# A decode block's backward pass: stores issued by SP, loads by GpSimd, and the turn's row products in another order

## The chip, the cores and the metric

The kernel runs on one core of a Trainium2 chip. A core has five engines with their own instruction queues: TensorE (PE), VectorE (DVE), ScalarE (ACT), GpSimd (POOL) and SyncE (SP, which only issues transfers and waits). Sixteen DMA engines move data between HBM and the on-chip memory (SBUF); a transfer is issued by SP, ScalarE or GpSimd, and the issuing engine works through its queue in order. The metric is the device time of one execution in microseconds. A profile of one execution is taken beside the timed runs.

## The reference

One token of a transformer block with adaptive layer norm, forward and backward. Cut to what matters here:

```python
mod = (silu(c) @ w_mod).reshape(1, 6, 1, -1)           # sa, ca, ga, sb, cb, gb
h = layernorm(x) * (1 + ca) + sa
q = (h @ wq) per head                                   # 32 heads, 192 each
p = softmax(q @ k_cache.T * 192 ** -0.5)                # 8192 keys per head
x1 = x + ga * ((p @ v_cache) @ wo)
h = layernorm(x1) * (1 + cb) + sb
out = x1 + gb * (h + gelu(layernorm(h) @ w3) @ w4)      # the mixing part before w3 falls away for one token
# outputs: out, and by jax.vjp the gradients of
# x, k_cache, v_cache, wq, wo, w3, w4, c, w_mod
```

All tensors are bfloat16. K and V are 32 x 8192 x 192 each, 100.7 MB; so are dK and dV. For one query, dV of a head is the outer product of p and the head's gradient do (8192 x 192), and dK the outer product of dS and q. dWo, dWq, dWmod, dW3 and dW4 are outer products of two vectors too.

## The kernel before

**Forward.** For each head, K is loaded in two halves (tiles of 128 x 32 x 192, 1.5 MB), multiplied by q on VectorE, summed by TensorE, and softmaxed; K scaled by p (tile EK) goes through TensorE with V. That gives the output o and, in MA_all and MB_all, the products that later yield dq without a second pass over K. All loads are issued by SP.

**The turn.** Between the last head's forward and the first head's backward lies a chain of small steps on 5 or 12 columns: the sum ao_c over the heads' products with Wo (`fwd_ao_add`), two layer norms (`ln_cols`), u = h W3, the GELU and its derivative, du, dn2 = du W3^T, two layer norm gradients (`ln_bwd_cols`), dao, the first pair's do, its broadcast do_pb, and the first dV. Beside this chain some bigger work is spread, in an order written by hand:

- `dg_some(n)`: row products on VectorE, one for each of the 12 blocks of W4 (a 128 x 640 product with a sum, into a column of d_g; needed for du);
- `w3T_pe(n)` and `w3T_act(n)`: 15 groups of transposes of W3 on TensorE into PSUM banks, and their copies by ScalarE (needed for dn2). Banks "a" and "b" hold one group, a tile of "s" two; which group takes which is `g % 6`;
- `woT_some(n)`: 4 groups of transposes of the last pair's Wo (needed for do).

These are called from the fills of the layer norms (`ln1_fill`, `ln2_fill`, `lb2_fill`), which run while the chain waits for a sum over partitions on TensorE.

**Backward.** One step i for each head, from the last to the first. In it (lines of the profile):

1. `bwd_mult` (L132, L1000): V of the head times do_pb on VectorE, in place, and sums by TensorE into dP_ps;
2. `ring_load`: loads into a ring of 6 tiles that hold V and, five times, a batch of Wo; a load waits for the reader of the tile that it replaces. The first three are issued ahead of the backward pass;
3. `bwd_dv` of the next head: 20 of 32 rows on ScalarE (L1005), 12 on VectorE (L983), and a store (L1008) for each half;
4. side work: the row products with Wo (L917), `job_dwo` in steps 1 to 16 (three products on ScalarE at L1050 and a store, L1069), `job_dw4` in steps 17 to 20 (L1058), `job_dw3` (L1063), and from step 9 on the pieces of Wq and Wmod: a load (`job_outer_load`, L1096), a product and stores of dWq and dWmod (wq_o, wm_o, L1125);
5. `bwd_ds` and `bwd_dk` (L983, L1035): the two halves of dK, each with a store.

dK, dV and the forward's K share five tiles ("big"); late in the backward more tiles join. All loads are issued by SP (`nc.sync`), all stores by GpSimd (`st2 = nc.gpsimd`). Each queue is in program order: a store that waits for its producer holds up the stores behind it, a load that waits for a free tile holds up the loads behind it.

Of the kernel before, what the change touches and what calls it, by code (L numbers as in the profile page):

```python
# [20 lines left out]
def kernel(  # L21
# [26 lines left out]
    nc = tc.nc  # L48
# [16 lines left out]
    P = 128  # L65
# [6 lines left out]
    JH = J // 2  # L72
# [21 lines left out]
    def bank(tag, bufs=1, name=None, n=512):  # L94
        return psum[0].tile([P, n], FP32, tag=tag, name=name or "ps_" + tag, bufs=bufs)
# [32 lines left out]
    def ccol(n, name, dtype=FP32):  # L128
        return const.tile([P, n], dtype, name=name)
# [195 lines left out]
            return (0, P), (P, DH), 0, 3 * (h // 2), 3 * (h // 2) + 1  # L325
        return (DH - P, DH), (0, DH - P), DH - P, 3 * (h // 2) + 2, 3 * (h // 2) + 1

    def load_v(pool, h, t, slot):
        tl = pool.tile([P, JH, DH], BF16, name="V_sb", tag=f"v{slot}")
        nc.sync.dma_start(out=tl, in_=V_hd[h][:, t * JH : (t + 1) * JH, :])  # L330
        return tl

    def load_fwd(h, t, kind):
# [205 lines left out]
    def dg_some(n):  # L539
        f0 = dg_next[0]  # L540
        f1 = min(f0 + n, NFC)
        dg_next[0] = f1
        for f in range(f0, f1):
            j0 = 5 * D + 12 * P + f % 2 * D
            jk = w_t[2][:, j0 : j0 + D]
            nc.vector.tensor_tensor_reduce(out=jk, in0=w4n(f, 0, D), in1=dbo_bc, scale=1.0, scalar=0.0, op0=ALU.mult, op1=ALU.add, accum_out=d_g[:, f : f + 1])
# [142 lines left out]
    def w3T_pe(n):  # L689
        for g in range(w3T_next[0], min(w3T_next[0] + n, NG3)):  # L690
            b = g % 6
            if b in (0, 2):
                w3T_ps[g] = bank("s", 2, "t_ps", SB[0])
                w3T_ps[g + 1] = w3T_ps[g][:, 512:1024]
            elif b > 3:
                w3T_ps[g] = bank("ab"[b - 4], name="t_ps")
            for k in range(4):
                f, i = divmod(4 * g + k, NDC)
                nc.tensor.matmul(w3T_ps[g][:, k * P : (k + 1) * P], lhsT=w3n(i, f * P, (f + 1) * P), rhs=ident_bf, start=True, stop=True)
        w3T_next[0] += n  # L700
# [18 lines left out]
    fwd_kvK(hl - 1, 3, st[hl - 1])  # L719
    nc.scalar.copy(out=kb_sb, in_=kb_ps[:, 0 : 2 * DH])  # L720
    fwd_ao_add(HH - 2, sl_["sm"])
    dg_some(1)
    fwd_ao_add(HH - 1, sl_["sm"], 420)
    fek_cm.__exit__(None, None, None)
    fsm_cm.__exit__(None, None, None)
# [13 lines left out]
    for i in range(1, HQ):  # L739
        ring += [("v", HS[i], t) for t in range(2) if (i, t) != (1, 1)]  # L740
        if i % 2 == 1 and 0 < i // 2 < len(BATCHES):
            ring.append(("w", i // 2, 0))
    ring_n, freed = [0], set()
    NR = 6

    def ring_slot(n):
        return (3, 4, 5, 2, 0, 1)[n % NR]

    def ring_load():
        while ring_n[0] < len(ring) and (ring_n[0] < 3 or ring_key(ring_n[0] - NR) in freed):  # L750
            kind, k, t = ring[ring_n[0]]
            slot = ring_slot(ring_n[0])
            pool = bv if slot > 2 else fv
            ring_n[0] += 1
            if kind == "v":
                V_b.setdefault(k, {})[t] = load_v(pool, k, t, slot)
            else:
                load_wo(k, pool.tile([P, JH, DH], BF16, name="V_sb", tag=f"v{slot}"))

    def load_wo(k, tl):  # L760
        lo, n = PS[BATCHES[k][-1]], len(BATCHES[k])
        tl = tl.rearrange("p j d -> p (j d)")[:, 0 : 3 * n * D].rearrange("p (c r) -> p c r", r=D)
        nc.sync.dma_start(out=tl, in_=wo_v[:, 3 * lo : 3 * (lo + n), :])
        for hp in range(lo, lo + n):
            for cc in range(3):
                wo_src[hp, cc] = tl[:, 3 * (hp - lo) + cc, :]
# [3 lines left out]

    ring_load()
    big_order[:] = [0, 4, 1, 4, 1, 2, 3, 4, 1, 2, 3, 4, 0, 1] + [2, 3, 4, 0, 1] * HQ
    st2 = nc.gpsimd

    do_pb = {}
    q_pb = {}
# [12 lines left out]
        bwd_pf_dve(h)  # L789

    def ln1_fill(k):
        if k == 0:
            dg_some(1)
        else:
            w3T_pe(4)
            w3T_act(4)

    def ln2_fill(k):
        w3T_pe(1 + 2 * k)
        dg_some(1)  # L800

    x1_c = ccol(NDC, "x1_c")
    mul(x1_c, ao_c, ga)
# [50 lines left out]
    for f in range(NFC):  # L854
        for i in range(NDC):
            nc.tensor.matmul(dn2_ps[:, i : i + 1], lhsT=w3T(f * NDC + i), rhs=du_bf[:, f : f + 1], start=False, stop=(f == NFC - 1), skip_group_check=True)
    bwd_pf_act(HS[0])
    dn2 = ccol(NDC, "dn2")
    dve_copy(dn2, dn2_ps[:, 0:NDC])
    mid_ps = {"h2": aux_ps[:, 32 : 32 + NDC]}  # L860
# [4 lines left out]
                nc.tensor.matmul(mid_ps["h2"][:, r : r + 1], lhsT=w4n(f, r * P, (r + 1) * P), rhs=g_bf[:, f : f + 1], start=False, stop=(f == 6), skip_group_check=True)  # L865

    def lb2_fill():
        woT_some(4)

    dhb = ccol(NDC, "dhb")  # L870
    ln_bwd_cols(dn2, n2_c, r2, dbo_c, dhb, "lb2", lb2_fill)
    dn1 = ccol(NDC, "dn1")
    mul(dn1, dhb, cb1)
    dx1 = ccol(NDC, "dx1")
    ln_bwd_cols(dn1, n1_c, r1, dy_c, dx1, "lb1")
    dao_bf = ccol(NDC, "dao_bf", BF16)
    mul(dao_bf, dx1, ga)
    bwd_pf_dve(HS[0])
# [175 lines left out]
    def job_dw4(k):  # L1054
        o = bso.tile([P, 3, D], BF16, name="dw4", tag="so")
        for cc in range(3):
            tsc(o[:, cc, :], dbo_bc, g_f[:, 3 * k + cc : 3 * k + cc + 1], 0)
        st2.dma_start(out=out_7[3 * k * P : 3 * (k + 1) * P, :].rearrange("(c p) r -> p c r", p=P), in_=o)  # L1058

    def job_dw3(i):  # L1060
        o = bso.tile([P, F], BF16, name="dw3", tag="so")
# [3 lines left out]
    def job_dwo(hp):  # L1065
        o = bso.tile([P, 3, D], BF16, name="dwo", tag="so")
        for cc in range(3):
            tsc(o[:, cc, :], dao_bc, o_col_f[:, 3 * hp + cc : 3 * hp + cc + 1], 0)
        st2.dma_start(out=out_5[3 * hp * P : 3 * (hp + 1) * P, :].rearrange("(c p) r -> p c r", p=P), in_=o)  # L1069

    side = {}
    side_cm = []
# [249 lines left out]
```

## Time and profile before

| | |
|---|---|
| median of three runs | 1381.44 us (1379.0 to 1411.71) |
| the profiled execution | 1382.5 us, span 1380.7 us |
| busy: TensorE / VectorE / ScalarE / GpSimd | 852.1 / 1070.6 / 945.0 / 112.0 us |
| moved over DMA | 569.25 MB, mean 412 GB/s |
| read from HBM / written to HBM | 341.51 / 225.91 MB |
| HBM rate, 36 to 500 us (forward) | 417 GB/s |
| HBM rate, 566 to 572 us (in the turn) | 96 GB/s |
| HBM rate, 660 to 1080 us (backward) | 425 GB/s |

The span is from the first to the last instruction; times within it are counted from its start. "Busy" of an engine counts its instructions' durations. The DMA share is the mean busy share of the 16 DMA engines. A wait is put down to what ended it. The forward pass ends at about 540 us, the first store of dV is issued at 570.93 us.

### The profile page before, as it was taken

How to read it: one execution, taken by the hardware profiler on the slowest of the kernel's cores; microseconds unless marked ns; L12 is line 12 of the kernel's file. 1: busy time of each engine (PE TensorE's matmuls, PEld its weight loads, DVE VectorE, ACT ScalarE, POOL GpSimd, SP SyncE). 2: the span in 40 equal slices, each digit the busy share in tenths (PEclk: the TensorE clock that was granted, in tenths of full speed). 3: DMA queues.
4: the chain of work that ended last, by engine and by line, in shares of the span. 5: the costliest groups of instructions: out<-in, count | busy, mean ns of one | idle time of the engine just before them, and what ended most of it. 6: DMA issues, size and time to landing. Idle time of an engine off the chain costs nothing. (4 is left out here: it accounts for less than half of the span.)

```text
span 1380.7 us, 28348 instructions
## 1 busy us (share of the span) xinstructions
PE 852.1 (62%) x11655; PEld 672.8 (49%) x11655; DVE 1070.6 (78%) x1273; ACT 945.0 (68%) x2586; POOL 112.0 (8%) x203
## 2 busy tenths in 40 slices
PE   3699999999999999738645744234332435324242
PEld 3577777777777777726534532123221323213131
DVE  3588778878887886799997977857757859579695
ACT  1388777877877884866786657576864866557781
POOL 0000000000000000111101101111111111021010
PEclk9799999999999998566666666666766666666665
DMA  9999999999999999899999999999999999999997
GB/s 392 416 415 420 419 418 420 421 411 418 418 419 407 418 417 376 311 381 422 409 425 427 427 426 428 428 426 427 420 423 421 407 427 426 429 423 406 429 428 311
DMA packets 73167, 569.25 MB, mean 412 GB/s; under 512 B 6862, under 2 KB 19918, under 8 KB 32846
## 3 DMA queue, kind: packets, MB, share of 16 engines
q1 hardware_dynamic: 48592, 341.52, 60.2%
q0 software_dynamic: 24416, 225.92, 38.9%
q8 instruction: 91, 1.49, 0.4%
q14 instruction: 38, 0.31, 0.1%
q10 hardware_dynamic: 30, 0.00, 0.0%
HBM read 341.51 MB, written 225.91 MB: 411 GB/s over the span
## 5 line engine op out<-in xcount | busy, mean ns | idle before, releaser
L1005 ACT ACTIVATE dV<-do_pb,PF 128x192 bf16<-128x192 bf16 x1246 | 434.6, 440 | 108.7 <-DMA out_dram<-dK 60.6
L1000 PE MATMUL dP_ps<-V_sb,ident_bf 128*128 128x256 bf16 (+1 forms) x1584 | 229.2, 319 | 246.8 <-DVE V_sb L132 246.8
L407 ACT ACTIVATE EK<-K_sb,E_f 128x192 bf16<-128x192 bf16 x992 | 351.1, 442 | 4.1 <-PE kb_ps L302 2.8
L1000 PEld LDWEIGHTS <-ident_bf 128*128 128x128 bf16 x1584 | 179.3, 116 | 296.3 <-issue 169.1
L983 DVE TENSOR_TENSOR dK<-dS,q_pb 128x6144 bf16<-128x6144 bf16 x64 | 213.2, 3354 | 59.4 <-DMA out_dram<-dK 54.0
L132 DVE TENSOR_TENSOR prod<-K_sb,q_pb 128x6144 bf16<-128x6144 bf16 x64 | 214.4, 3349 | 3.6 <-DMA K_sb<-in_A_k_cache_dram 3.6
L132 DVE TENSOR_TENSOR V_sb<-V_sb,do_pb 128x6144 bf16<-128x6144 bf16 (+1 forms) x66 | 212.0, 3253 | 0.0
L432 PE MATMUL ps_a<-EK,V_sb 128*128 128x193 bf16 x1984 | 192.9, 249 | 1.9 <-DMA V_sb<-in_A_v_cache_dram 1.9
L432 PEld LDWEIGHTS <-V_sb 128*128 128x128 bf16 x1984 | 165.6, 99 | 19.5 <-issue 12.7
L983 DVE TENSOR_TENSOR dV<-P2h,do_pb 128x2304 bf16<-128x2304 bf16 (+2 forms) x67 | 88.8, 1353 | 50.1 <-DMA out_dram<-dV 40.4
L414 DVE TENSOR_TENSOR EK<-K_sb,P2h 128x1536 bf16<-128x1536 bf16 x124 | 117.5, 949 | 0.0
L1008 POOL DMA_DIRECT2D out_dram<-dV x68 | 37.0, 545 | 934.9 <-DVE dV L983 607.7
L443 PE MATMUL ps_b<-EK,V_sb 128*64 128x193 bf16 x1984 | 109.3, 253 | 0.0
L372 PE MATMUL S_ps<-prod,ident_bf 64*64 64x256 bf16 x3072 | 101.7, 280 | 11.9 <-DVE prod L132 11.9
L372 PEld LDWEIGHTS <-ident_bf 64*64 64x64 bf16 x3072 | 86.7, 111 | 32.6 <-issue 28.3
L443 PEld LDWEIGHTS <-V_sb 128*64 128x64 bf16 x1984 | 81.9, 110 | 19.7 <-issue 16.1
L393 ACT ACTIVATE E_f<-sm_ps,negm 128x64 f32<-128x64 f32 x31 | 9.7, 314 | 104.4 <-DVE negm L391 104.4
L376 DVE TENSOR_REDUCE S<-S_ps 128x128 f32<-128x1024 f32 x32 | 39.2, 1224 | 49.0 <-PE S_ps L372 49.0
L449 PE MATMUL kb_ps<-EK,hot_bf 128*32 128x384 bf16 x992 | 64.8, 339 | 0.0
L1050 ACT ACTIVATE wq_o<-wq_bc,ha_f 128x1536 bf16<-128x1536 bf16 x12 | 18.4, 1564 | 44.4 <-DMA out_dram<-wq_o 44.4
L191 PE MATMUL bc_ps<-ident_bf,dq_bf 128*128 128x128 bf16 x48 | 6.4, 304 | 66.6 <-ACT do_pb L195 65.5
L1035 POOL DMA_DIRECT2D out_dram<-dK x64 | 35.3, 552 | 136.7 <-DVE dK L983 95.1
(266 smaller groups left out, 805.8 us busy)
## 6 DMA issues: line engine op xcount, KB each, us to landing
V_sb<-in_A_v_cache_dram SPq DMA_DIRECT2D x125, 1536.0 KB, 14.2
K_sb<-in_A_k_cache_dram SPq DMA_DIRECT2D x64, 1536.0 KB, 14.4
out_dram<-dK POOLq DMA_DIRECT2D x64, 1536.0 KB, 23.0
out_dram<-dV POOLq DMA_DIRECT2D x61, 1536.0 KB, 22.4
wq<-in_A_wq_dram SPq DMA_DIRECT2D x3, 2560.0 KB, 33.9
wo_t<-in_A_wo_dram SPq DMA_DIRECT2D x16, 480.0 KB, 14.9
out_dram<-dwo POOLq DMA_DIRECT2D x16, 480.0 KB, 18.2
wq<-in_A_wq_dram SPq DMA_DIRECT2D x4, 1920.0 KB, 28.3
```

What stands on the lines that cost most here:

```text
L132: nc.vector.tensor_tensor(out=out, in0=a, in1=b, op=ALU.mult)
L372: nc.tensor.matmul(st["S_ps"][c0 : c0 + 64, r, t * JH : (t + 1) * JH, :], lhsT=ident_bf[64 * r : 64 * r + 64, 64 * r : 64 * r + 64], rhs=p ...
L376: nc.vector.reduce_sum(out=st["S2"], in_=st["S_ps"], axis=AX.X)
L407: nc.scalar.activation(out=st["EK"][q][:, jj, 0:DH], in_=K_st[h, t][:, r * JQ + jj, :], func=ACT.Copy, scale=st["E_f"][:, j : j + 1])
L414: nc.vector.tensor_tensor(out=EK[:, NA:JQ, 0:DH].rearrange("p j (d r) -> p j d r", r=2), in0=K_st[h, t][:, r * JQ + NA : (r + 1) * JQ, :]. ...
L432: nc.tensor.matmul(st["A_ps"][:, 0:n], lhsT=V_sb[:, r * JQ + jj, a0:a1], rhs=EK[:, jj, 0:n], start=(q == 0 and jj == 0), stop=(q == 3 and ...
L443: nc.tensor.matmul(st["B_ps"][g : g + 64, 0:n], lhsT=V_sb[:, r * JQ + jj, b0:b1], rhs=EK[:, jj, 0:n], start=(q == 0 and jj < 2), stop=(q = ...
L449: nc.tensor.matmul(kb_ps[g : g + 32, 0 : 2 * DH], lhsT=hot_bf[:, HQ - 1 - h : 2 * HQ - 1 - h], rhs=EK[:, jj : jj + 2, 0:DH], start=(h == 0 ...
L983: nc.vector.tensor_tensor(out=o.rearrange("p j (d r) -> p j d r", r=2), in0=pairs[:, :, None, :].to_broadcast([P, n, NP2, 2]), in1=vec.rea ...
L1000: nc.tensor.matmul(bst[h]["dP_ps"][:, t * JH + r : t * JH + r + n, :], lhsT=ident_bf, rhs=V_sb[:, :, k * DS : (k + 1) * DS], start=(k == 0 ...
L1005: nc.scalar.activation(out=o[:, jj, :], in_=vec_of(do_pb, h), func=ACT.Copy, scale=bst[h]["PF"][:, t * JH + jj : t * JH + jj + 1])
L1008: st2.dma_start(out=dV_hd[h][:, t * JH + r0 : t * JH + r1, :], in_=o[:, r0:r1, :])
```

## The change

The stores of dK, dV, dW3, dWq, dWmod and of the small outputs move from GpSimd's queue to SP's; the loads of the ring from the fourth on, all loads of Wo for the backward pass, and those of Wq and Wmod move from SP's queue to GpSimd's. The stores of dWo and dW4 stay on GpSimd. In the turn, one row product leaves the place between the two additions to ao_c, one leaves the first fill of ln2, and one joins the second fill of ln1; W3's groups of transposes take the PSUM banks in another order (a, b first, then the double ones); Wo's transposes are spread over three places: one group ahead of the copy of dn2, two in the fill of the first layer norm gradient, one in that of the second.

```diff
-    def load_v(pool, h, t, slot):
+    def load_v(pool, h, t, slot, eng=None):
         tl = pool.tile([P, JH, DH], BF16, name="V_sb", tag=f"v{slot}")
-        nc.sync.dma_start(out=tl, in_=V_hd[h][:, t * JH : (t + 1) * JH, :])
+        (eng or nc.sync).dma_start(out=tl, in_=V_hd[h][:, t * JH : (t + 1) * JH, :])
...
     def w3T_pe(n):
             b = g % 6
-            if b in (0, 2):
+            if b in (2, 4):
...
-            elif b > 3:
-                w3T_ps[g] = bank("ab"[b - 4], name="t_ps")
+            elif b < 2:
+                w3T_ps[g] = bank("ab"[b], name="t_ps")
...
     fwd_ao_add(HH - 2, sl_["sm"])
-    dg_some(1)
     fwd_ao_add(HH - 1, sl_["sm"], 420)
...
+    ldq = nc.gpsimd
...
-                V_b.setdefault(k, {})[t] = load_v(pool, k, t, slot)
+                V_b.setdefault(k, {})[t] = load_v(pool, k, t, slot, ldq if n >= 3 else nc.sync)
...
     def load_wo(k, tl):
-        nc.sync.dma_start(out=tl, in_=wo_v[:, 3 * lo : 3 * (lo + n), :])
+        nc.gpsimd.dma_start(out=tl, in_=wo_v[:, 3 * lo : 3 * (lo + n), :])
...
-    st2 = nc.gpsimd
+    st2 = nc.sync
...
     def ln1_fill(k):
-        if k == 0:
-            dg_some(1)
-        else:
+        dg_some(1)
+        if k == 1:
             w3T_pe(4)
             w3T_act(4)
...
     def ln2_fill(k):
         w3T_pe(1 + 2 * k)
-        dg_some(1)
+        dg_some(k)
...
     bwd_pf_act(HS[0])
+    woT_some(1)
     dn2 = ccol(NDC, "dn2")
...
     def lb2_fill():
-        woT_some(4)
+        woT_some(2)
+
+    def lb1_fill():
+        woT_some(1)
...
-    ln_bwd_cols(dn1, n1_c, r1, dy_c, dx1, "lb1")
+    ln_bwd_cols(dn1, n1_c, r1, dy_c, dx1, "lb1", lb1_fill)
...
     def job_dw4(k):
-        st2.dma_start(out=out_7[3 * k * P : 3 * (k + 1) * P, :].rearrange("(c p) r -> p c r", p=P), in_=o)
+        nc.gpsimd.dma_start(out=out_7[3 * k * P : 3 * (k + 1) * P, :].rearrange("(c p) r -> p c r", p=P), in_=o)
...
     def job_dwo(hp):
-        st2.dma_start(out=out_5[3 * hp * P : 3 * (hp + 1) * P, :].rearrange("(c p) r -> p c r", p=P), in_=o)
+        nc.gpsimd.dma_start(out=out_5[3 * hp * P : 3 * (hp + 1) * P, :].rearrange("(c p) r -> p c r", p=P), in_=o)
...
     def job_outer_load(name, view, lo, n):
-        nc.sync.dma_start(out=w, in_=view[:, :, lo : lo + n])
+        ldq.dma_start(out=w, in_=view[:, :, lo : lo + n])
```

More of the change, by code (lines that the diff above doesn't have):

```diff
@@ L750, in ring_load @@
         while ring_n[0] < len(ring) and (ring_n[0] < 3 or ring_key(ring_n[0] - NR) in freed):
-            kind, k, t = ring[ring_n[0]]
-            slot = ring_slot(ring_n[0])
+            n = ring_n[0]
+            kind, k, t = ring[n]
+            slot = ring_slot(n)
             pool = bv if slot > 2 else fv
```

## The prediction

> **What bounds the kernel now.** I read the page's slices of DMA first, then a table of stretches, then waits and issues, and last the turn's timeline.
>
> ```profile
> DMA  9999999999999999899999999999999999999997
> DMA packets 73167, 569.25 MB, mean 412 GB/s; under 512 B 6862, under 2 KB 19918, under 8 KB 32846
> q1 hardware_dynamic: 48592, 341.52, 60.2%
> q0 software_dynamic: 24416, 225.92, 38.9%
> ```
>
> The first line is the busy share of the 16 DMA engines in 40 slices, in tenths: full from start to end, with a notch at the turn and one at the end. All loads are in the first queue (issued by SP), all stores in the second (issued by GpSimd); together they fill the engines. By stretches (start and end in us, the length, busy time of the five engines, granted clock, DMA share, GB/s):
>
> ```profile
> 36.00:500.00 464.00, 433.91 (x7864) 342.60 (x7857) 370.59 (x559) 352.91 (x1040) 0.00 (x0) 0.97 1.01 417
> 540.00:566.00 26.00, 22.78 (x419) 20.74 (x419) 16.81 (x76) 13.86 (x30) 0.00 (x0) 0.61 0.97 376
> 566.00:572.00 6.00, 4.36 (x93) 3.89 (x91) 3.52 (x10) 3.63 (x12) 0.88 (x2) 0.50 0.27 96
> 572.00:600.00 28.00, 15.18 (x250) 14.49 (x251) 27.69 (x32) 19.93 (x58) 4.61 (x9) 0.62 0.97 371
> 660.00:1080.00 420.00, 183.74 (x1117) 141.08 (x1117) 325.35 (x301) 287.29 (x727) 58.21 (x100) 0.65 1.01 425
> 1321.00:1360.00 39.00, 14.49 (x96) 11.10 (x96) 38.65 (x22) 28.85 (x84) 4.79 (x9) 0.71 1.01 426
> 1371.00:1380.70 9.70, 0.00 (x0) 0.00 (x0) 0.00 (x0) 0.00 (x0) 0.00 (x0) 0.50 0.07 30
> ```
>
> The backward pass moves 425 GB/s at a share of 1.01, whatever its engines wait for. Idle transfer time is only in the turn (566 to 572) and behind 1371. So a change of who issues a transfer can pay in three ways only: packets that take another time, a shorter turn, a better end. The waits (line waited at, what for, total us, times, longest) and the issues (count, size, median us to landing):
>
> ```profile
> SPq L330 <- DVE V_sb L132: 397.1, 29, 28.2
> POOL out_dram L1069 <- ACT dwo L1050: 75.8, 10, 19.7
> V_sb<-in_A_v_cache_dram SPq DMA_DIRECT2D x125, 1536.0 KB, 14.2
> out_dram<-dK POOLq DMA_DIRECT2D x64, 1536.0 KB, 23.0
> ```
>
> SP waits for a free V slot most of the time, so loads go out as early as slots allow. In the timeline the last pair of V loads goes out at 1290.8 and 1293.4 and is multiplied at 1343.8 and 1347.0; the fourth load of the ring goes out at 583.9 for a product at 642.1. A load thus leads its use by 53 to 58 us and lands in 14.2 (longest 27.9): 25 us to spare at the least.
>
> **The sum, part by part.** Durations are those of the profiled execution (1382.5 us, span 1380.7), 1.1 over the median of the runs shown.
>
> *Stores of dK, dV, dW3, Wq and Wmod from GpSimd to SP.* That is 64 dK, 68 dV, 5 dW3, 20 wq_o, 15 wm_o: 216 MB by the issue table. The trace's packet records give 463 ns for a 12,288-byte packet of the store queue and 472 ns for one of SP's queue (424 and 416 GB/s over 16 engines). But one queue only writes HBM and the other only reads it, so the trace can't say whether the 2% belong to the queue or to the direction. If to the queue, the stores take 216/416 - 216/424 = 10 us more, and the V loads (58 of 1.573 MB = 91 MB) 91/416 - 91/424 = 4 us less: +6. If to the direction: 0. Nothing excludes that SP's stores run better than either, so the other end is -6. Far off, SP's 12,288-byte packets ran at 387 GB/s in 540 to 600, among short rows; at that rate the stores would cost 216/387 - 216/424 = 49. I take 0: the stretch nearest to it is 1321 to 1360, stores alone, at the same 426 as the mix. Short rows: the store queue joins them (6,144 bytes 243 ns, 5,120 bytes 197 ns), SP's queue sends each alone (3,072 bytes 122 ns, 2,560 bytes 102 ns). Two SP packets take 244 for 243 (wq_o, dW3), and 204 for 197 (wm_o, 960 pairs, 960 x 7 / 16 engines = 0.4 us). On their new queue SP, these stores stand behind nothing but each other: SP's loads are gone from it after the third of the ring. What ends the wait for a buffer is a landing, and that is set by the full engines.
>
> *Loads of V, Wo, Wq, Wmod from SP to GpSimd.* Wo has rows of 1,280 bytes; from SP each is a packet of 55 ns. 5 loads hold 5,376 rows: 5,376 x 55.1 ns / 16 = 18.5 us. If GpSimd joins four as it does for dWo (5,120 bytes in 197 ns), 1,344 x 197 / 16 = 16.6: a gain of 1.9, against 0 if it does not join loads. I take 1.9, as its only queue with such rows shows it. Wq: 0; Wmod 0.4 gained, which cancels wm_o's.
>
> The loads now share GpSimd's queue with dWo and dW4. In each of the first 16 steps a dWo store waits there for ScalarE, and the next step's V loads stand behind it: 75.8 us in 10 waits, the longest 19.7, which 25 us of cover hide. Without cover the excess falls on VectorE's product with V, then on dP, dS, dK. The reverse is a gain on paper: dK no longer waits behind dWo. But in the widest such hole, 711.6 to 729.5, with no store issued, the transfers held 421 to 429 GB/s. I take 0.
>
> *The turn.* These rows set it (start, us, engine, line):
>
> ```profile
> 549.23 0.82 DVE L546 CUSTOM_DVE_ANT_0 w_t<-w_t,dbo_bc 128x640 bf16<-128x640 bf16 x1
> 549.97 0.16 DVE L135 TENSOR_TENSOR ao_c<-ao_c,sm_ps 128x5 f32<-128x5 f32 x1
> 552.86 0.16 DVE L168 RECIPROCAL ln_rstd<-ln_std 128x1 f32<-128x1 f32 x1 [1.03 <-ACT ln_std L165]
> 561.38 1.47 PE L856 MATMUL kb_ps<-du_bf,w3T_t 128*128 128x1 bf16 x48
> 566.90 0.16 DVE L132 TENSOR_TENSOR lb_t<-ln_n,lb_m 128x5 f32<-128x5 f32 x1 [1.12 <-PE lb_m L150]
> 570.93 0.68 POOL L1008 DMA_DIRECT2D out_dram<-dV  x1 [569.28 <-DVE dV L983]
> ```
>
> The row product at 549.23 stands between the two additions to ao_c, although TensorE has both sums by 549.2: moved away, 549.97 - 549.23 = 0.74 gained. Its new place is the 1.03 us of idle ahead of the reciprocal (552.86), which holds its 0.82. ln2's first product leaves a place that was hidden, for the late group: two products instead of one ahead of the last column of du, 0.75 more. That is covered: TensorE starts on du at 561.38 only because W3's transposes end there, and comes to the last two of its 12 groups of 5 columns some 1.6 us later. If that cover went, it costs up to 0.75. In the two LayerNorm gradients, the wait for lb_m is 0.68 the first time and 1.12 the second, where Wo's transposes stand ahead of it; spread over three places they leave it at 0.68 or so: 0.4. The order of PSUM banks for W3 frees the same groups before the same users: 0.
>
> The first dV store: VectorE's first piece ends about 570.5 (8 of the 64 rows that five pieces take 6.83 us for), GpSimd begins at 570.93 and bytes flow at 572.0. SP's first load of all goes out at 0.75 and bytes flow at about 1.75, so the way is as long; a nearer start may give 0 to 0.4, and I take 0.2. The first GpSimd load, Wo at 561.5, lands for use at 606: late by 1 us it costs nothing. The turn gives 0.74 + 0.4 + 0.2 = 1.3, all of it real, because the engines have nothing to move until that store.
>
> Sum: 1382.5 - 1.9 - 1.3 = 1379.3; less the 1.1 to the median, **1378**.
>
> **Rivals.** *Lag of one engine (gain).* Behind 1371 the table shows 30 GB/s, about one engine's sixteenth of 426 (27): one engine works alone for some 7 us. The completion counts of the stores say the same: the last of 16 comes 0.3 us behind the fifteenth at 600 to 700, 1.7 at 900 to 1000 and 6.5 from 1300 on. If it is the store queue's descriptors that slow this engine, stores from SP end together: 7 - 7/16 = 6.5 us less, 1378 - 6.5 = 1372. Against it: in the forward pass, with SP alone, the first of the 16 stands 5 to 7 us ahead of the last too. The Trainium skill (DMA: Bandwidth & Descriptors, Latency and other measured facts) calls two of the 16 engines usually slower, with GpSimd's descriptor rings as its best guess and SP free of it; the trace agrees that one engine is late, and can't show which.
>
> *Rate goes with the queue (loss).* The +6 above: 1384.
>
> *Late loads (slower than before).* Loads move to the queue with the longer landings, whose longest was 34.6 for dK, and behind dWo's wait of 19.7. 34.6 + 19.7 = 54.3 against a lead of 53: the mechanism decides as soon as landings pass 53 - 19.7 = 33 us. Then each of the 20 steps with a dWo or dW4 store loses the excess, VectorE's product waits for V, and with it the stores: 20 x 1.3 = 26 us; with the longest landing of a Wo load, 36.1, it is 20 x 2.8 = 56. So 1404 to 1434, in the middle 1419. For it: a queue whose issuer waits for ScalarE. Against it: 23.0 was the landing of a queue with four 1.5 MB stores for each head, and the loads are two; only 10 of the 16 dWo stores waited. GpSimd's issue itself took 532 ns at the median and 895 at most for dV, with VectorE 75% busy. The Trainium skill (SBUF — State Buffer, SBUF: two separate sides) speaks against this half of the change: VectorE in its two-port modes locks GpSimd out and descriptors can't be written, about 620 ns becoming 3100. The 895 ns bound does not show it.
>
> *All starvation gone (large gain).* Bringing 540 to 660 (3.0 + 4.6 + 3.6, and 398 GB/s from 600 to 660, 3.8) and the dips at 1080 (366 GB/s for 10 us, 1.4) and 1250 (388 for 20, 1.7) to 425, and the lag of 6.5, adds up to 24.6: 1382.5 - 24.6 = 1358 at the very best. Over 2% is more than the profile has to give.
>
> **How the numbers follow.** Chances: forecast 0.54 (own range 1374 to 1382), rate with the queue 0.10, lag gone 0.12, late loads 0.17, SP's far rate 0.01, and 0.06 for gains that the profile has no place for. About 2%, 28 us, is what a measurement of this kernel can tell from no change: faster is below 1354, slower above 1409. Faster 0.06; slower 0.14, SP's far rate and 0.13 of the late loads, whose lower end lies below 1409; within 0.80. The range runs from 1358, all starvation gone, to 1409, with that lower end in it: what is left out is 0.06 + 0.14.
>
> **What would show it.** Right: the backward stretches stay at 420 to 430 GB/s with a share near 1; Wo packets of 5,120 bytes in GpSimd's queue; the first dV store 1 to 1.5 us earlier; loads still 50 us ahead. Wrong: 12,288-byte packets of SP's stores away from 463 ns by over 5%; idle of VectorE ahead of its product with V put down to a V load; the tail behind the last full slice shorter or longer than 7 us.

## The result, and the profile after

The changed kernel takes 1391.94 us (median of 20 runs, 1380.39 to 1396.11), the kernel before 1381.87 (median of 20, 1377.64 to 1411.71): a ratio of 1.0068, 95% interval 1.0055 to 1.0081. That is slower by 9 to 10 us: less than 2%, but clear of the interval, where the forecast was a gain. Of the 20 runs two took 1380.39 and 1383.19 us and the other 18 between 1387.41 and 1396.11, so not every execution has the loss. The profiled execution took 1388.9 us, 3 below the median, and its span is 1387.1; what follows accounts for this execution, 6.4 us over the span before.

The table of stretches, as before the change (start and end in us, the length, busy time of the five engines, granted clock, DMA share, GB/s):

```profile
566.00:572.00 6.00, 4.97 (x97) 4.73 (x94) 4.35 (x10) 3.97 (x12) 0.00 (x0) 0.50 0.63 231
572.00:600.00 28.00, 14.55 (x248) 13.73 (x248) 27.69 (x33) 19.93 (x58) 1.08 (x2) 0.62 0.92 355
600.00:660.00 60.00, 35.74 (x233) 30.19 (x232) 58.35 (x88) 43.33 (x119) 5.78 (x8) 0.67 1.00 405
660.00:1080.00 420.00, 179.36 (x1072) 137.74 (x1072) 317.23 (x296) 277.77 (x703) 36.36 (x55) 0.65 1.00 414
1080.00:1320.00 240.00, 91.52 (x589) 66.78 (x589) 181.56 (x113) 166.88 (x444) 14.06 (x24) 0.66 1.01 421
```

The stretch 660 to 1080 moved 425 GB/s and now moves 414: 420 x 11 / 425 = 10.9 us of transfers left over for later. Of the others, 566 to 600 moved 362 KB more (0.9 us gained), 600 to 660 went from 398 to 405 GB/s (1.0 gained), 1080 to 1320 from 422 to 421 (0.6 lost). At the end, behind 1371, the engines stood empty for 9.0 us' worth of transfers before and for 6.1 now, most of it behind 1380 (2.9 gained). Together 10.9 + 0.6 - 0.9 - 1.0 - 2.9 = 6.7, and the span is 6.4 longer; the stretches ahead of 566 and from 1320 to 1371 differ by about 1 us each at most, both ways. The loss has one main place, then, the stretch in which most of dWo and dW4 is stored. In slices of 20 us:

```profile
920.00:940.00 20.00, 5.60 (x16) 2.17 (x16) 9.80 (x5) 9.82 (x20) 1.70 (x2) 0.59 1.00 405
940.00:960.00 20.00, 7.00 (x54) 5.72 (x54) 18.26 (x14) 16.08 (x43) 1.87 (x3) 0.67 0.92 363
960.00:980.00 20.00, 8.01 (x60) 6.57 (x60) 13.91 (x7) 10.36 (x25) 0.89 (x2) 0.62 0.93 380
980.00:1000.00 20.00, 8.23 (x43) 5.07 (x43) 17.78 (x12) 18.53 (x45) 1.89 (x3) 0.74 0.99 397
```

Before the change the same four slices had 425, 428, 422 and 421 GB/s; the middle two:

```profile
940.00:960.00 20.00, 1.86 (x15) 1.56 (x15) 12.85 (x4) 8.14 (x16) 2.43 (x4) 0.54 1.01 428
960.00:980.00 20.00, 9.50 (x63) 6.49 (x62) 14.66 (x9) 19.86 (x48) 3.47 (x6) 0.84 1.01 422
```

After the change the share falls to 0.92 and 0.93 there: some DMA engines have nothing to do, where before every slice from 660 to 1320 had a share of 0.99 or more. Who waits at that time shows in the timeline, ScalarE's first (start, length, engine, line, and in brackets the idle time ahead and what ended it):

```profile
929.49 0.34 ACT L782 ACTIVATE PF<-E_all,rinv_bc 128x64 f32<-128x64 bf16 x1
942.83 13.92 ACT L1009 ACTIVATE dV<-do_pb,PF 128x192 bf16<-128x192 bf16 x40 [13.01 <-DMA out_dram<-dK]
956.66 2.25 ACT L1054 ACTIVATE dwo<-dao_bc,o_col_f 128x640 bf16<-128x640 bf16 x3
969.09 1.57 ACT L1054 ACTIVATE wq_o<-wq_bc,ha_f 128x1536 bf16<-128x1536 bf16 x1 [10.18 <-DMA out_dram<-wq_o]
```

and VectorE's:

```profile
934.06 6.63 DVE L987 TENSOR_TENSOR dK<-dS,q_pb 128x6144 bf16<-128x6144 bf16 x2 [10.16 <-DMA out_dram<-dV]
```

ScalarE waits 13 us and VectorE 10 us for a tile that is still being stored. A store has landed only when its last DMA engine is done. The times at which the 16 parts of one transfer complete show how far the engines have drifted apart (issued between 800 and 900; first part to last, median and longest, of the transfers whose parts the trace tells apart, 28 of 32 and 18 of 28):

```
                 transfers   median    longest
before                  28    5.2 us    11.3 us
after                   18   15.9 us    22.0 us
```

Of SP's stores issued between 800 and 1100 in the changed kernel, the first fourteen parts complete within 4.2 us of one another at the median, the last two 6.6 and 9.5 us behind them: one or two engines are behind. That fits the waits: the engines ahead have finished their share of everything issued, and a tile comes back only with the engine that is behind. It is argued, as the trace doesn't say which engine a part or a packet belongs to.

Empty engines are the smaller part of the loss. Worked out from the packet records between 660 and 1080 us, as a mean per DMA engine, the time without a packet went from 0.1 to 4.0 us (3.5 of it in the two slices above), and the time that packets took over the median of their size from 2.7 to 10.3: 3.9 us more of empty engines, 7.6 more of slow packets. A packet of 12,288 bytes takes 460 ns at the median in both kernels and on both queues; between 660 and 1080 the mean went from 463 to 471 ns, and the share of packets over 600 ns from 0.7% to 2.9%.

The waits of GpSimd now hold the loads, as the prediction listed them (line waited at, what for, total us, times, longest):

```profile
POOL V_sb L330 <- PE dP_ps L1004: 320.9, 32, 28.7
POOL out_dram L1073 <- ACT dwo L1054: 129.1, 10, 28.0
```

75.8 us in 10 waits became 129.1 in 10, the longest 19.7 became 28.0, with V loads behind it. Yet VectorE's product with V does not wait; the page's group of that line (busy us, mean ns, then the idle time ahead):

```profile
L132 DVE TENSOR_TENSOR V_sb<-V_sb,do_pb 128x6144 bf16<-128x6144 bf16 (+1 forms) x66 | 212.0, 3253 | 0.4 <-DMA V_sb<-in_A_v_cache_dram 0.4
```

0.4 us in 66 products: no load came late. The queues and the landings:

```profile
DMA packets 69518, 569.26 MB, mean 410 GB/s; under 512 B 6796, under 2 KB 14476, under 8 KB 29196
q1 hardware_dynamic: 54990, 446.72, 77.5%
q0 software_dynamic: 14368, 120.72, 21.5%
...
out_dram<-dK SPq DMA_DIRECT2D x64, 1536.0 KB, 23.2
...
V_sb<-in_A_v_cache_dram POOLq DMA_DIRECT2D x58, 1536.0 KB, 18.4
out_dram<-dwo POOLq DMA_DIRECT2D x16, 480.0 KB, 21.4
```

Packets under 2 KB fell from 19,918 to 14,476: 5,376 rows of Wo now travel in packets of four. A V load takes 18.4 us to land on GpSimd's queue, 44.5 at the longest. The 14.2 on SP's queue before is no measure for that, as 64 of its 125 loads belong to the forward pass: those of the backward pass took 16.7 at the median, 27.9 at the longest (37 of 58 can be told). dK's landing is unchanged (23.2 for 23.0).

The turn, in VectorE's and then SP's timeline:

```profile
549.30 0.35 DVE L135 TENSOR_TENSOR ao_c<-ao_c,sm_ps 128x5 f32<-128x5 f32 x2 [0.81 <-PE sm_ps L520]
...
552.40 0.16 DVE L168 RECIPROCAL ln_rstd<-ln_std 128x1 f32<-128x1 f32 x1 [0.29 <-ACT ln_std L165]
...
566.06 0.16 DVE L132 TENSOR_TENSOR lb_t<-ln_n,lb_m 128x5 f32<-128x5 f32 x1 [0.74 <-PE lb_m L150]
...
568.83 6.83 DVE L987 TENSOR_TENSOR dV<-P2h,do_pb 128x1536 bf16<-128x1536 bf16 x5 [0.95 <-ACT do_pb L354]
```

```profile
569.81 9.30 SPq L1012 DMA_DIRECT2D out_dram<-dV  x7
```

From the reciprocal of the last softmax (545.37, before 545.21) to the first dV product it is 23.46 us for 24.45: 1.0 shorter. The first store follows its product's start by 0.98 instead of 1.27.

### The profile page after: what moved, and what is told of

Read it like the earlier page. It is cut to its first block, busy times and chain, and to the rows that moved or that the text cites. A ratio compares the mean times of both kernels' runs of the same rounds, so it can differ in the third digit from the quotient of the medians.

```text
span 1387.1 us, 28374 instructions
## 1 busy us (share of the span) xinstructions
PE 857.7 (62%) x11655; PEld 677.1 (49%) x11655; DVE 1070.6 (77%) x1273; ACT 945.0 (68%) x2586; POOL 59.5 (4%) x98
## 2 busy tenths in 40 slices
DMA packets 69518, 569.26 MB, mean 410 GB/s; under 512 B 6796, under 2 KB 14476, under 8 KB 29196
## 5 line engine op out<-in xcount | busy, mean ns | idle before, releaser
L1004 PE MATMUL dP_ps<-V_sb,ident_bf 128*128 128x256 bf16 (+1 forms) x1584 | 234.5, 324 | 232.8 <-DVE V_sb L132 232.7
L1004 PEld LDWEIGHTS <-ident_bf 128*128 128x128 bf16 x1584 | 182.1, 118 | 285.1 <-issue 162.1
L432 PEld LDWEIGHTS <-V_sb 128*128 128x128 bf16 x1984 | 168.0, 100 | 19.8 <-issue 12.7
L443 PEld LDWEIGHTS <-V_sb 128*64 128x64 bf16 x1984 | 80.7, 109 | 19.6 <-issue 15.9
L1054 ACT ACTIVATE wq_o<-wq_bc,ha_f 128x1536 bf16<-128x1536 bf16 x12 | 18.4, 1566 | 48.4 <-DMA out_dram<-wq_o 48.4
L330 POOL DMA_DIRECT2D V_sb<-in_A_v_cache_dram x58 | 31.5, 544 | 419.3 <-PE dP_ps L1004 320.9
L1115 PEld LDWEIGHTS <-ident_bf 128*128 128x128 bf16 x112 | 13.6, 122 | 68.9 <-issue 64.7
## 6 DMA issues: line engine op xcount, KB each, us to landing
out_dram<-dK SPq DMA_DIRECT2D x64, 1536.0 KB, 23.2
V_sb<-in_A_v_cache_dram POOLq DMA_DIRECT2D x58, 1536.0 KB, 18.4
out_dram<-dwo POOLq DMA_DIRECT2D x16, 480.0 KB, 21.4
```

The costliest lines, as they stand in the source:

```text
L330: (eng or nc.sync).dma_start(out=tl, in_=V_hd[h][:, t * JH : (t + 1) * JH, :])
L432: nc.tensor.matmul(st["A_ps"][:, 0:n], lhsT=V_sb[:, r * JQ + jj, a0:a1], rhs=EK[:, jj, 0:n], start=(q == 0 and jj == 0), stop=(q == 3 and ...
L443: nc.tensor.matmul(st["B_ps"][g : g + 64, 0:n], lhsT=V_sb[:, r * JQ + jj, b0:b1], rhs=EK[:, jj, 0:n], start=(q == 0 and jj < 2), stop=(q = ...
L1004: nc.tensor.matmul(bst[h]["dP_ps"][:, t * JH + r : t * JH + r + n, :], lhsT=ident_bf, rhs=V_sb[:, :, k * DS : (k + 1) * DS], start=(k == 0 ...
```

## The experiments

All ratios are to the kernel before, measured on the same chip beside each run. "Lost" is worked out from the profiled execution's packet records between 660 and 1320 us, as a mean per DMA engine: the time without a packet, and what packets took over the median of their size (460 ns for 12,288 bytes, 196 for 5,120, 55 for 1,280). GpSimd also has Wo's loads except where the table says none.

| run | GpSimd's queue in the backward pass | ratio, 95% | span | lost, us |
|---|---|---|---|---|
| before | all stores; no loads | | 1380.7 | 6.8 |
| after | loads, dWo/dW4 | 1.0068 [1.0055, 1.0081] | 1387.1 | 18.3 |
| e13_after_again | the same kernel again | 1.0075 [1.0048, 1.0101] | 1387.7 | 18.8 |
| e1_turn_only | all stores; no loads | 0.9996 [0.9987, 1.0005] | 1380.2 | 7.3 |
| e2_all_sp | dWo/dW4; no loads | 0.9998 [0.9988, 1.0008] | 1379.8 | 5.9 |
| e3_all_pool | all loads, all stores | 1.0053 [1.0039, 1.0067] | 1387.9 | 15.9 |
| e4_loads_alone | loads | 0.9999 [0.9989, 1.0009] | 1379.6 | 9.2 |
| e5_dwo_later | loads, dWo/dW4 a step later | 1.0079 [1.0054, 1.0105] | 1382.2 | 11.7 |
| e6_wait_no_bytes | loads, and a wait for ScalarE | 1.0029 [1.0017, 1.0042] | 1386.0 | 13.9 |
| e7_wo_loads_gpsimd | Wo's loads, dWo/dW4 | 0.9986 [0.9977, 0.9994] | 1379.2 | 6.8 |
| e16_wo_again | the same kernel, another chip | 0.9989 [0.9977, 1.0000] | 1378.0 | 5.2 |
| e8_all_gpsimd_dwo_sp | all loads, stores but dWo/dW4 | 1.0015 [0.9995, 1.0034] | 1383.0 | 8.6 |
| e9_long_rows | loads, dWo/dW4 in 3,840-byte runs | 0.9998 [0.9989, 1.0007] | 1382.4 | 12.5 |
| e10_ready_rows | loads, ready rows for dWo/dW4 | 1.0008 [0.9997, 1.0019] | 1380.2 | 10.9 |
| e14_ready_held | e10 and the wait for ScalarE | 1.0013 [1.0001, 1.0025] | 1382.8 | 13.9 |
| e11_wo_alone | Wo's loads | 1.0005 [0.9984, 1.0026] | 1382.8 | 9.2 |
| e12_other_rows | loads, dWq/dWmod/dW3 | 1.0130 [1.0112, 1.0147] | 1396.2 | 20.6 |
| e15_other_ready | loads, ready rows for dWq/dWmod/dW3 | 1.0088 [1.0065, 1.0111] | 1391.7 | 23.1 |

Every span above 1387 goes with more than 15 us lost there, and every span up to 1383 with less than 14: the time follows the lost transfer time, though roughly (e6 and e14 both lost 13.9, with spans 3.2 us apart; e15 lost more than e12 in a shorter span). The profiled run of e5, 1383.98, was the lowest of its six, the others took 1393.53 to 1397.33: its trace shows the program without most of its loss.

**Which part of the change costs it.** Four kernels first: the turn alone; the stores on SP with the loads left there; the loads on GpSimd with the stores left there; and the change without dWo and dW4 on GpSimd.

```diff
 e1_turn_only
-    ldq = nc.gpsimd
+    ldq = nc.sync
...
-        nc.gpsimd.dma_start(out=tl, in_=wo_v[:, 3 * lo : 3 * (lo + n), :])
+        ldq.dma_start(out=tl, in_=wo_v[:, 3 * lo : 3 * (lo + n), :])
...
-    st2 = nc.sync
+    st2 = nc.gpsimd
```

> The changed kernel with both queues as before (all backward loads on SP, all stores on GpSimd); only the turn's row products, banks and Wo transposes are reordered. All theories: the turn alone is about 1 us faster than before (ratio 0.999). If instead the turn's order costs later, the ratio would be 1.003 or more.

```diff
 e2_all_sp: ldq = nc.sync and load_wo on ldq as in e1, st2 stays nc.sync
 e3_all_pool: st2 = nc.gpsimd, loads as in the changed kernel
 e4_loads_alone, in job_dwo and likewise in job_dw4:
-        nc.gpsimd.dma_start(out=out_5[3 * hp * P : 3 * (hp + 1) * P, :].rearrange("(c p) r -> p c r", p=P), in_=o)
+        st2.dma_start(out=out_5[3 * hp * P : 3 * (hp + 1) * P, :].rearrange("(c p) r -> p c r", p=P), in_=o)
```

> The changed kernel with the backward loads back on SP beside the stores; only dWo and dW4 stay on GpSimd. Theory A (each transfer that changes its queue gets slower packets, stores 4 us in all, loads 4 us in all, independently): +3 us over before (4 less 1 for the turn), ratio 1.002. Theory B (what costs is the company in a queue, loads that wait for a slot and stores or dWo that wait for ScalarE in one order, which bunches the transfers until single DMA engines lag): worse than the changed kernel, ratio 1.01 or more, since stores stand behind loads. Theory C (only SP's stores cost): as the changed kernel, 1.007.

> The changed kernel with the stores back on GpSimd beside the loads; SP has no transfer of the backward pass after the first three loads. Theory A: +3 us less 2 us for Wo rows sent in packets of four, ratio 1.001 to 1.002. Theory B: worse than the changed kernel, 1.01 or more. Theory C (only SP's stores cost): 0.998 to 1.000.

> The changed kernel with dWo and dW4 stored from SP too, so that GpSimd has loads alone and no load stands behind a store that waits for ScalarE. Theory A: no gain, plus up to 2 us for dWo's rows of 1,280 bytes sent singly by SP: ratio to before 1.007 to 1.008. Theory B with dWo as the company that costs: the loss goes, 1.000 to 1.002. Theory C: 1.007 or a little more.

None of the three theories had e2 or e3 right, and e4 came out beside theory B's case for dWo. Moving the big stores to SP costs nothing (e2: 0.9998). Moving the loads to GpSimd costs nothing either, as long as they are alone there (e4: 0.9999). The loss comes with dWo and dW4 in the queue of the loads: taking these 20 small stores out of it, 9.8 MB of the 569, takes it away whole. In e4's stretches:

```profile
660.00:1080.00 420.00, 181.06 (x1126) 141.93 (x1126) 322.73 (x300) 288.33 (x730) 23.86 (x40) 0.65 1.01 424
1080.00:1320.00 240.00, 91.24 (x587) 66.11 (x584) 182.56 (x111) 157.69 (x422) 11.87 (x21) 0.67 1.00 418
```

424 GB/s again in the stretch that had lost it, and the parts of a transfer issued between 800 and 900 land within 3.0 us (median of 19; longest 7.3) where the changed kernel has 15.9. The mean 12,288-byte packet is 464 ns on either queue there, so neither queue has a rate of its own there.

**Wait or bytes.** The obvious reading is the hold: V loads stand behind a store that waits for ScalarE. e5 issues the same store a step later, behind that step's loads; e6 leaves the wait and takes the bytes away.

```diff
 e5_dwo_later
-        nc.gpsimd.dma_start(out=out_5[...], in_=o)
+        owed.append(lambda: nc.gpsimd.dma_start(out=out_5[...], in_=o))
...
         ring_load()
+        while owed:
+            owed.pop(0)()
 e6_wait_no_bytes (on top of e4)
+        nc.gpsimd.tensor_copy(out=seen, in_=o[:, 2, 0:1])
         st2.dma_start(out=out_5[...], in_=o)
```

> The changed kernel, with each dWo and dW4 store still issued by GpSimd but one step later, right behind that step's V loads, when ScalarE has long finished it: no load stands behind a wait for ScalarE, the bytes in each queue stay the same. Theory H (the wait ahead of the loads costs): ratio to before 1.000 to 1.002, time of engines idle and slow packets between 660 and 1080 us gone. Theory M (stores and loads mixed in GpSimd's queue make packets slow, wait or no wait): as the changed kernel, 1.006 to 1.008.

> dWo and dW4 are stored from SP (as in the run with GpSimd's loads alone, 0.9999), but at their place GpSimd copies one column of the finished dWo tile, so that the next loads wait for ScalarE as in the changed kernel, without a byte of dWo in GpSimd's queue. Theory H: the loss is back, 1.005 to 1.008. Theory M: 1.000 to 1.001.

e5 turned out to be no clean test: GpSimd runs so far ahead that it still stood at that store for ScalarE, 110.9 us in 9 waits, and 1.0079 says only that the place in the program doesn't cure it. In e6 the wait is there in full:

```profile
POOL V_sb L330 <- PE dP_ps L1004: 297.4, 32, 30.6
POOL seen L1076 <- ACT dwo L1054: 162.5, 16, 26.9
```

162.5 us in 16 waits, more than in the changed kernel, for 1.0029: about two fifths of the loss, between the two cases expected. It also falls elsewhere, 3.4 us of empty engines in one slice that the changed kernel passes at 426 GB/s:

```profile
720.00:740.00 20.00, 16.60 (x97) 14.81 (x96) 19.76 (x23) 13.01 (x35) 2.69 (x4) 0.67 0.84 323
```

Two more of this group put stores and loads together in other ways.

```diff
 e7_wo_loads_gpsimd: ldq = nc.sync (load_wo stays on nc.gpsimd)
 e8_all_gpsimd_dwo_sp: st2 = nc.gpsimd, and in job_dwo and job_dw4
-        nc.gpsimd.dma_start(out=out_5[...], in_=o)
+        nc.sync.dma_start(out=out_5[...], in_=o)
```

> The backward's stores and its V, Wq and Wmod loads on SP, GpSimd with the five Wo loads and with dWo and dW4. Beside the run with all loads on SP (0.9998) the rows of Wo go out as packets of 5,120 bytes. Theory H: GpSimd's Wo loads stand behind dWo's waits, but five of them only: 0.998 to 1.000 (1.9 us of packet time gained). Theory M: the same mixture in GpSimd's queue in small: 1.000 to 1.002.

> All loads and the big stores on GpSimd (1.0053 with dWo there too), dWo and dW4 alone on SP. Theory H: loads still stand behind dV stores that wait for ScalarE, dWo's wait is gone: 1.003 to 1.005. Theory M (mixing of loads and stores in GpSimd's queue): 1.005 or more. If dWo's short rows in GpSimd's queue are what slows its loads: 1.000 to 1.001.

e8 against e3 is the cleanest pair: with all loads and all big stores on GpSimd, moving dWo and dW4 alone from GpSimd to SP takes 1.0053 down to 1.0015, with intervals that don't overlap. Most of what is left may be the rows: SP sends dWo and dW4 as 7,680 packets of 1,280 bytes where GpSimd sends 1,920 of 5,120, by the medians 20 x (384 x 55 - 96 x 196) / 16 = 2.9 us more, 0.2%. And e7, which has dWo and dW4 on GpSimd but the V loads not, is faster than both kernels: they do no harm in a queue without V loads.

**What it is about these stores.** e9 stores them in longer runs, e10 stores rows that are ready from the start (nothing to wait for), e11 takes them off GpSimd in e7, e12 puts other short-row stores into the queue of the loads.

```diff
 e9_long_rows
-        ....rearrange("(c p) r -> p c r", p=P), in_=o)
+        ....rearrange("(p c) r -> p c r", c=3), in_=o)
 e10_ready_rows (dW4: dbo_bc)
-        ....rearrange("(c p) r -> p c r", p=P), in_=o)
+        ....rearrange("(c p) r -> p c r", p=P), in_=dao_bc[:, None, :].to_broadcast([P, 3, D]))
 e11_wo_alone: e7 with dWo and dW4 on nc.sync
 e12_other_rows: e4, and in job_outer_out (likewise in job_dw3)
-        st2.dma_start(out=dram[i * P : (i + 1) * P, lo : lo + n], in_=o)
+        nc.gpsimd.dma_start(out=dram[i * P : (i + 1) * P, lo : lo + n], in_=o)
```

> The changed kernel, but dWo and dW4 are stored with 3,840 bytes in one run for each partition instead of three rows of 1,280: the same bytes, the same queue, the same wait for ScalarE, fewer descriptors; the rows of dWo and dW4 come to lie in another order than the reference's. If the loss comes from the hold (the V loads stand behind a store that waits for ScalarE): still 1.005 to 1.008 of the time before. If it comes from the short rows that GpSimd's queue gathers out of four partitions each: 0.998 to 1.002.

> The changed kernel, but GpSimd stores rows that are ready from the start of the loop (the broadcast gradient without its factor) in place of dWo and dW4: bytes, rows, queue and place in the program unchanged, ScalarE still computes its products, and no store waits for them; dWo and dW4 are therefore not the reference's. If the loss is the hold: no wait of GpSimd for ScalarE over 2 us, ratio 0.998 to 1.002. If it is the store's bytes among the V loads in GpSimd's queue: 1.004 to 1.008. Both with a share each: 1.003 to 1.005, since the wait without bytes cost 0.29%.

> All stores and the loads of V, Wq and Wmod on SP; GpSimd has the five loads of Wo and nothing else in the backward pass. If Wo's joined rows (1.9 us worked out) and the turn (1.3) are real gains and nothing else counts: 0.997 to 0.999, as with dWo and dW4 on GpSimd (0.9986). If dWo and dW4 on SP, as packets of 1,280 bytes (20 stores of 384 rows at 55 ns against 96 at 197 ns: 1.4 us over 16 engines), give that back: 0.9985 to 1.0005.

> Loads alone on GpSimd (0.9999 of before), with the stores of dWq, dWmod and dW3 added to GpSimd's queue: rows of 2,560 and 3,072 bytes that GpSimd joins by twos, most of them from 1,000 us on, behind products of ScalarE or VectorE. If every store that waits there holds up loads: a loss of 0.2 to 0.8%, seen in the stretch 1080 to 1320 too (below 421 GB/s). If only dWo's kind of store or its place ahead of the V loads counts: 0.999 to 1.001.

e9 gives 0.9998 with GpSimd still waiting for ScalarE nearly as long as in the changed kernel (121.0 us in 10 waits, the longest 23.5), and dWo and dW4 in 1,280 packets of 7,680 bytes instead of 1,920 of 5,120: the hold makes no loss there.

```profile
POOL out_dram L1073 <- ACT dwo L1054: 121.0, 10, 23.5
```

e10 gives 1.0008 with the bytes, rows and packets unchanged and no hold. e12 gives the largest loss of all, 1.0130, and in another stretch (dWo and dW4 are on SP here):

```profile
660.00:1080.00 420.00, 176.22 (x1063) 136.14 (x1060) 311.24 (x288) 278.30 (x703) 34.34 (x59) 0.65 1.01 420
1080.00:1320.00 240.00, 90.31 (x594) 65.76 (x593) 179.97 (x115) 157.75 (x421) 23.58 (x42) 0.67 0.99 405
```

405 GB/s from 1080 to 1320, where the changed kernel has 421: the loss moves to the steps that store dWq and dWmod. So e9 speaks for the rows and e10 for the hold, each against the other. e11, at 1.0005 with an interval of 0.4%, doesn't decide between its two cases; the second was worked out too small, as its own terms give 2.8 us and not 1.4, and with 2.8 it lies about 1.0006, where the run is.

**Both together.** After these, hold and short rows together were left as an explanation. e14 puts the hold back into e10, e15 takes it out of e12; the changed kernel and e7 ran again beside them.

```diff
 e14_ready_held (on top of e10)
+        nc.gpsimd.tensor_copy(out=seen, in_=o[:, 2, 0:1])
         nc.gpsimd.dma_start(out=out_5[...], in_=dao_bc[:, None, :].to_broadcast([P, 3, D]))
 e15_other_ready (on top of e12; dW3 likewise)
-        nc.gpsimd.dma_start(out=dram[i * P : (i + 1) * P, lo : lo + n], in_=o)
+        nc.gpsimd.dma_start(out=dram[i * P : (i + 1) * P, lo : lo + n], in_=du_bc[:, 0:n])
```

> The changed kernel unchanged, measured beside the next three. If its loss is a property of the program and not of the chip that first ran it: 1.004 to 1.010. If runs without loss belong to it as much: an interval that reaches 1.002.

> The kernel that stores ready rows in place of dWo and dW4 (1.0008), with one thing put back: ahead of each of these stores GpSimd copies one column of ScalarE's last product, so that the store and the V loads behind it wait for ScalarE again (dWo and dW4 are not the reference's). If the loss needs wait and short rows together: 1.004 to 1.009. If the wait costs by itself what it cost without the bytes: 1.002 to 1.004. If it is neither (the buffer that ScalarE gets back only after the store has landed): 0.999 to 1.002.

> The kernel with dWq, dWmod and dW3 on GpSimd's queue beside the loads (1.013), but storing rows of a broadcast that is ready (these three outputs are therefore not the reference's). Same bytes, rows and queue. If the loss comes from loads held behind products: 0.999 to 1.003, and 1080 to 1320 back at 420 GB/s or more. If it comes from the short rows by themselves: 1.008 to 1.015, and about 405 GB/s as before.

> Loads of V, Wq and Wmod and the stores on SP, with Wo's loads and the stores of dWo and dW4 on GpSimd, once more, beside the changed kernel. If the gain is the program's: 0.997 to 0.9995. If it was the scatter between one measurement and the next: 0.9995 to 1.002.

That explanation fell too. e14 has the hold and the rows:

```profile
POOL V_sb L330 <- PE dP_ps L1004: 330.1, 33, 28.7
POOL seen L1076 <- ACT dwo L1054: 116.1, 13, 19.7
```

and costs 1.0013, about what e10 costs without the hold (its longest wait is 19.7 us, the changed kernel's 28.0). e15 has no hold for ScalarE, and still costs 1.0088:

```profile
660.00:1080.00 420.00, 172.68 (x1037) 133.56 (x1036) 300.80 (x276) 268.59 (x684) 43.41 (x77) 0.64 1.00 411
1080.00:1320.00 240.00, 95.54 (x618) 69.08 (x615) 191.54 (x130) 168.80 (x447) 13.41 (x24) 0.68 1.00 416
```

In most of these runs the drift of the engines goes with the loss. First part to last of the transfers issued between 800 and 900 (medians; stores issued by SP, transfers issued by GpSimd):

```
                     SP        GpSimd     ratio
after              15.4 us    15.9 us    1.0068
e13_after_again    19.4 us    14.1 us    1.0075
e15_other_ready    15.3 us    12.9 us    1.0088
e9_long_rows       12.7 us     7.9 us    0.9998
e14_ready_held      9.9 us     2.3 us    1.0013
e10_ready_rows      7.8 us     2.2 us    1.0008
e6_wait_no_bytes    3.4 us     3.8 us    1.0029
e4_loads_alone      3.6 us     2.8 us    0.9999
```

(e12 drifts later, 15.2 us on SP's stores between 1000 and 1100, and stands empty for 5.4 us between 1080 and 1320.) Where SP's stores drift by 15 us, the engines stand empty for 3.5 to 4.4 us between 660 and 1080 (after, e13, e15); at 12.7 (e9) it is 1.4, and below that 0.5 at most, but for e6's one slice.

The drift can't be the whole cause, and e3, which is not in that list, shows it best. It lost 0.53%, and its 32 transfers issued between 800 and 900 (all GpSimd's) land within 6.3 us at the median, 6.7 at the most; before, they were 5.2 and 11.3. Its DMA engines are hardly ever short of work, with a share of 1.01:

```profile
660.00:1080.00 420.00, 190.51 (x1129) 145.25 (x1127) 321.04 (x298) 289.06 (x729) 81.22 (x137) 0.65 1.01 416
```

Of its 15.9 us lost, 15.4 are slow packets; in the changed kernel it is 14.2 of 18.3, before 6.3 of 6.8. In every profile with a span above 1387, then, slow packets are the larger part, and empty engines come on top where the drift is large. e13 has the slices of the changed kernel nearly unchanged (364 and 388 GB/s from 940 to 980 for its 363 and 380): the episode belongs to the program, if not to every execution of it.

**What stays open.** In these runs the large losses (0.5% and more) come only with short-row stores and V loads in GpSimd's queue together; the runs without one or the other lie within 0.15% of before by their ratios (e11 0.16% by its median), but for e6 with its wait. Such a queue may also run with little or no loss (e9, e10, e14, and e8, which has dWq, dWmod and dW3 among the loads). Not shown is what makes the packets slow, or what in a program sets off the drift. e14 differs from the changed kernel only in the tile the rows are read from, in what ScalarE's products then wait for (nothing in either), and in GpSimd's copy; why that keeps the engines together no run says.

**The version that beats both** is e7, by 0.1% over the kernel before, measured twice: 0.9986 and 0.9989 (the second interval ends at 1.0000), medians 1380.09 and 1379.70 us. Its stretches:

```profile
660.00:1080.00 420.00, 188.62 (x1130) 144.22 (x1130) 326.28 (x301) 294.79 (x746) 14.10 (x18) 0.65 1.01 425
1360.00:1371.00 11.00, 0.00 (x0) 0.00 (x0) 0.00 (x0) 0.00 (x0) 0.00 (x0) 0.50 0.81 346
1371.00:1378.00 7.00, 0.00 (x0) 0.00 (x0) 0.00 (x0) 0.00 (x0) 0.00 (x0) 0.50 0.05 21
```

(e16's profile.) Nothing is lost in the middle, and Wo's rows are joined.

## Why the prediction was wrong, point by point

- **The bound**, transfers at 425 GB/s and waits that don't matter, was right for the kernel before. The step that failed stands there: "So a change of who issues a transfer can pay in three ways only". It counted ways to gain, and its sum ends without a term for a loss. Two were open: the first of the three ways, packets that take another time, works downwards too, and engines can run dry in the middle of a full stretch. Between 660 and 1080 slow packets cost 7.6 us more than before and empty engines 3.9, more than the 3.2 us of gains in the sum.
- **Loads in one queue with dWo and dW4** were taken at 0, because "in the widest such hole, 711.6 to 729.5, with no store issued, the transfers held 421 to 429 GB/s". That row showed that a hold of stores is harmless while SP goes on issuing loads. It couldn't show the queue of the changed kernel, which had no row in the trace; e4 against the changed kernel prices it at 1.0068 - 0.9999 = 0.7%, 9.5 us. This is the term that made the forecast wrong; why the pair costs it stays open.
- **Late loads**, the rival on the slow side, had the right edit and the wrong mechanism. The hold grew to 28.0 us, 25 of cover were thus too few on paper, and still VectorE waited 0.4 us for V in all. The cover itself was misread: the lead of 53 to 58 us came from three loads, and over all 58, paired in order with their products, the least is 38 us before and 26 after (medians 60 and 61). What waited was ScalarE and VectorE, for tiles still being stored, 13 and 10 us at a time.
- **Stores on SP at 0**: right. e2, with the loads beside them, is at 0.9998, and the typical 12,288-byte packet is 460 ns on both queues. The 463 against 472 mixed stages, neither queue nor direction: between 660 and 1080 the kernel before has 463 ns for GpSimd's stores and 462 for SP's loads, while SP's loads took 470 in the forward pass (36 to 500) and 553 from 600 to 660. *Rate goes with the queue* falls with it, though its 1384 lay nearer the result than the forecast.
- **Wo's joined rows, 1.9 us**: the packets came as worked out. e7 and e2 differ in them alone: 0.9998 - 0.9986 = 0.0012, 1.7 us, with intervals of 0.0009 to 0.0010 either way on each, and again 1.2 us with e16's ratio: it fits 1.9, but is not clear of nothing. The changed kernel has these packets too, and its loss outweighs them.
- **The turn, 1.3 us**: 1.0 between reciprocal and dV for the 1.14 forecast, 0.3 on the first store for 0.2. The reciprocal's idle time shrank from 1.03 to 0.29 us as the row product moved there, the wait for lb_m from 1.12 to 0.74. As time it hardly shows: e1 gives 0.9996, which 1.1 of 1382 (0.0008) fits as well as nothing does.
- **Lag of one engine at the end**: the cause offered for it, the store queue's descriptors, falls. e7 has all big stores on SP and still ends with 7.0 us at 21 GB/s (e16's profile). The prediction saw this lag, gave it 0.12 as a gain at the end, and didn't ask what a larger lag would do in the middle, where it goes with the 3.9 us of empty engines. The rule cited from the Trainium skill (DMA: Bandwidth & Descriptors, Latency and other measured facts), two engines usually slow with GpSimd's descriptor rings as its best guess, isn't borne out either: with GpSimd holding nothing but Wo's loads (e11) SP's transfers issued between 800 and 1100 land within 6.5 to 7.0 us of first part to last, and with every transfer there on GpSimd (e3) the last part comes 0.3 us behind the fifteenth. The trace can't name the engines.
- **VectorE locking GpSimd out** (the Trainium skill, SBUF — State Buffer, SBUF: two separate sides): not seen in the issues. GpSimd's issue of a V load took 544 ns at the mean in 58, against 532 at the median for a store before.
- **The numbers**: 1378 with 1374 to 1382 for the likeliest case, a small gain; measured 1391.94, a loss. The whole range held it, and "within 2%" was the likeliest class, but that is the width of the range, and luck, as no case in it has what happened. The 2% that the prediction took as the least a measurement can tell was far too wide: the interval of this ratio is 0.26% from end to end.

## What to carry to other kernels

Where a stretch is bound by saturated transfers, ask of each edit what could make packets slower or leave a DMA engine without work, not only what could make packets faster: look at the packets over their median, and at the time from the first to the last part of a transfer, since a tile comes back with the last part. Don't mix short-row stores into GpSimd's queue with the big loads unless it has been measured; where the two were kept apart (big loads and stores on SP, short rows on GpSimd) the joined packets were a small gain. And where a longer wait stands beside a loss, put the wait back alone: here that cost 0.3% in one kernel and 0.05% in another, of a loss of 0.7%.

## What the runs showed of the hardware that was not expected

- One transfer's 16 parts completed up to 24.8 us apart (e13, between 800 and 900), where the whole transfer lands in 23 us at the median; the changed kernel shows it in both of its profiles (22.0 in the other), and a change of the tile that 20 small stores read from (e10) brings it back to 9.8 at the most for SP's stores there.
- GpSimd joins rows of 1,280 bytes for loads as for stores: 5,120 bytes in 196 ns at the median, against 55 ns for each of four rows from SP. dWo, alone with Wo's loads in GpSimd's queue (e16), landed in 9.1 us; among the V loads it took 21.4.
- dWo's stores read from one ready tile (e10) landed in 33.6 us instead of 21.4, and the time was better all the same: the landing of a transfer that nobody waits for says nothing.
- Large packets got slower on average with both the typical packet (460 ns) and the busy share (1.01) unchanged: in e3 2.5% of the 12,288-byte packets between 660 and 1080 took over 600 ns, before 0.7%.
